# The last batch's rows leave in two pieces, and its gates are worked out ahead of other copies

## The chip, the cores and the metric

The kernel runs on one core of a Trainium2 chip. TensorE (PE) multiplies matrices into PSUM banks; VectorE (DVE) and ScalarE (ACT) read those banks and do the elementwise work; GpSimd (POOL) mostly issues DMAs here, among them all indirect ones; SyncE (SP) issues DMAs alone, and ACT can issue them too. Each engine works through its own instructions in the order in which they were written down. The metric is the device time of one execution in microseconds, the median of several.

## The reference

First chunked attention: 4 batches, 8 heads, 768 positions of 64 numbers, in chunks of 32 queries that see a window of 56 keys and 8 memory slots. Its result is laid out as 3,072 rows of 512. Then a mixture of 8 experts with two layers (512 to 1,024 to 512), in which each row goes to the two experts with the largest noisy logits:

```python
x = np.ascontiguousarray(attn_out.transpose(0, 2, 1, 3)).reshape(B * S, H * D)
logits = x @ w_gate
noisy_logits = logits + np.log1p(np.exp(x @ w_noise)) * noise
top2 = np.argpartition(-noisy_logits, 2, axis=1)[:, :2]
top2_w = np.exp(top2_l - top2_l.max(-1, keepdims=True))
top2_w /= top2_w.sum(-1, keepdims=True) + 1e-09
...
h = np.maximum(x[mask] @ w1[e], 0.0)
out[mask] += top2_w[mask, k, None] * (h @ w2[e])
```

## The kernel before

**Attention.** Sixteen pairs of heads (`NPAIR`, four to a batch) go through one software pipeline: transposes of q and k, scores, maximum, exponential, the product with v, and the division that writes the pair's columns into `xrow`, a tile of 128 partitions x 6 x 264 words per batch. A row of it has `XC` = 256 words for the 512 bf16 numbers and 8 words for the gates. `xT_pe` transposes a pair's columns on PE and copies them on ACT (tile `xt`); `logits_pe` multiplies `xt` with both gate matrices into `bankL`.

**Routing.** When a batch has its logits, `route(b)` gives a list of groups of steps. `s1` makes the noise scale (`ns`, two ACT instructions), `s1b` the noisy logits (`nl`), `s2` and `s2b` count for each expert how many beat it (`over`) and keep the two best (`two`, `mm_all`); `s3` ranks the rows by two-step prefix sums on PE; `s2c` and `s2d` make the exponentials (`gd` on DVE, `ge` on ACT); `s4` normalises them into the gates, stores them in the last 8 words of `xrow` and writes the batch's rows to `x_rows` in DRAM (L422); `s4b` and `s5` turn ranks into slots (`rk`, `r_all`, `past`, `tl`), `s5b` (`Rn`, DVE) and `s5c` (`col`, GpSimd) make the one-hot factors, `s6` multiplies them on PE, `s7` adds to the table `tab`. `decode` makes row numbers of the table: `idx_s` after batch 1, `idx_a` after batch 2, `idx_f` (with `idx_h`) after batch 3, the last.

**Experts.** The work is cut into ten sets: four tiles of 128 rows each for experts 0 and 1, filled from the first batches, then those experts' remaining three tiles, then seven tiles each for experts 2 to 7 (the seventh tile of an expert has 64 rows). For each set GpSimd gathers rows from `x_rows` by index (L604), `turn` transposes a tile on PE and copies it and its gate, `up` multiplies by w1 and `relu` evicts to `hts` or `htf`, `down` multiplies by w2, evicts with the gate as factor to `ys`, and GpSimd adds the rows to `out` by an indirect DMA (L676). The first scatter of a set waits until all of the set before has landed. `every()` is a generator over this; `units(k)` runs k of its yields (a yield is one block of 128 of the 1,024 hidden columns in `up`, or one tile in `down`), `until(mark)` runs it to a mark. `cnt["by"]` says which engine evicts: DVE, ACT, or both in turn.

**Order.** It is written out by hand: instructions stand on each engine as the program calls them. At the end of attention the last batch's routing is threaded through the first two sets, whose first halves were gathered by `idx_s` and whose second halves by `idx_a`. The groups of `route(B - 1)` run with (3, 4, 1, 4, 1) yields behind them, and three yields ahead. After the last group comes `decode` to `idx_f`, and then the gathers of all that is left. Tiles in DRAM carry dependencies: a batch's row write goes through a view of its own (`xd_part`), and gathers read through the whole of `x_rows`, so a gather waits for the row writes issued before it, and a row write for the gathers issued before it.

**Overflow.** Rows that find no slot are counted at the end; for them the gates are read back from `x_rows` (tile `gov`, L850, on SyncE), multiplied by what was missed and written back (L873), and a loop that normally does not run handles them.

Of the kernel before, what the change touches and what calls it, by code (L numbers as in the profile page):

```python
# [12 lines left out]
F32 = mybir.dt.float32  # L13
# [11 lines left out]
def kernel(  # L25
# [14 lines left out]
    nc = tc.nc  # L40
    B, H, S, D = q.shape
# [8 lines left out]
    NP = N // 128  # L50
# [9 lines left out]
    NT = 7  # L60
# [28 lines left out]
    def body():  # L89
# [231 lines left out]
        def mult_dve(n):  # L321
# [6 lines left out]
            nc.vector.reciprocal(rec.rearrange("p x u (h o) -> p x u h o", o=1), po[:, :, :, :, D:D + 1])  # L328
            nc.vector.tensor_tensor(out=xr, in0=po[:, :, :, :, :D], in1=rec.rearrange("p x u (h o) -> p x u h o", o=1).to_broadcast([128, 2, UB, 2, D]), op=Alu.mult)  # L329

        logits = {}

        def xT_pe(n):
            b, hp = divmod(n, HP)
            p_x = bf16v(tr(), BT, 128)
            for t in range(BT):
                nc.tensor.transpose(out=p_x[:, t, :], in_=xrows[b][:, t, hp * 64:(hp + 1) * 64].bitcast(BF16), identity=identb)
            xt = ap_.tile([128, BT, 128], BF16, name="xt")
            nc.scalar.copy(xt, p_x)
            st[n]["xt"] = xt  # L340

        def logits_pe(n):
            b, hp = divmod(n, HP)
            if hp == 0:
                logits[b] = f32v(bankL, BT, 2 * E)
            for t in range(BT):
                nc.tensor.matmul(out=logits[b][:, t, :], lhsT=st[n]["xt"][:, t, :], rhs=wgn[:, hp, :],
                                 start=(hp == 0 and t == 0), stop=(hp == KP - 1), skip_group_check=True)
# [5 lines left out]
        def route(b):  # L354
# [61 lines left out]
            def s4():  # L416
                ge, gs = R["ge"], T("gs", [128, BT])
                nc.vector.tensor_mul(ge, ge, R["two"])
                nc.vector.tensor_reduce(out=gs, in_=ge, axis=AX, op=Alu.add)
                nc.vector.reciprocal(gs, gs)  # L420
                nc.vector.tensor_tensor(out=xrows[b][:, :, XC:].bitcast(F32), in0=ge, in1=bc(gs, E), op=Alu.mult)
                (nc.sync if b < B - 1 else nc.scalar).dma_start(out=xd_part[b][b * S:(b + 1) * S].rearrange("(t p) r -> p t r", p=128), in_=xrows[b])  # L422

            def s4b():
                sh = [128, BT, 2, E]
# [62 lines left out]
                    nc.vector.tensor_add(seen[:, :EARLY], seen[:, :EARLY], gap)  # L488

            if b == B - 1:  # L490
                return (s1,), (s1b, s2), (s2b, s3, s2c, s4b, s5, s5c), (s2d,), (s4, s5b), (s6, s7)
            if b == B - 3:
                return (s1,), (s1b, s2), (s2b, s2c, s2d), (s3, s4, s4b, spare_a), (s5, s5c, spare_b), (s5b, spare_c), (s6, s7, s8, spare_d, begin_first)
            return (s1,), (s1b, s2), (s2b, s2c, s2d), (s3, s4, s4b), (s5, s5c), (s5b,), (s6, s7, s8)
# [239 lines left out]
        def units(k):  # L734
            for _ in range(k):
                next(moe, None)

        def until(*mark):
            for at in moe:
                if at == mark:  # L740
                    return
            assert False, mark
# [68 lines left out]
            zero_fill(8 * x, 8)  # L811
        load_w2(1)
        logits_pe(NPAIR - 2)
        xT_pe(NPAIR - 1)
        cnt["by"] = "dve"
        for j in range(FIRST):
# [1 line left out]
        logits_pe(NPAIR - 1)  # L818
        begin, *rest = route(B - 1)
        begin[0]()  # L820
        units(3)
        cnt["by"] = "act"
        for g, more in zip(rest, (3, 4, 1, 4, 1)):
            for fn in g:
                fn()
            units(more)
# [11 lines left out]
        actx.close()  # L838
        pools["full"] = ctx.enter_context(tc.tile_pool(name="full", bufs=1))
        lp = ctx.enter_context(tc.tile_pool(name="lp", bufs=1))  # L840
        until("down", NS - 4, NT - 1)


# [2 lines left out]
        sh = [128, NP, 2, E]  # L846
        miss = lp.tile(sh, F32, name="miss")
        nc.vector.tensor_tensor(out=miss, in0=mm_all, in1=o12.rearrange("p t (k o) -> p t k o", o=1).to_broadcast(sh), op=Alu.mult)
        gov = lp.tile([128, NP, E], F32, name="gov")
        nc.sync.dma_start(out=gov, in_=xd[:, XC:].rearrange("(t p) e -> p t e", p=128).bitcast(F32))  # L850
        nc.vector.tensor_add(miss[:, :, 0], miss[:, :, 0], miss[:, :, 1])
        nc.vector.tensor_mul(gov, gov, miss[:, :, 0])
        ov = lp.tile([128, NP], F16, name="ov")
# [108 lines left out]
```

## Time and profile before

| | |
|---|---|
| median of 3 runs | 346.19 us (344.0 to 346.33) |
| profiled execution: time, span | 343.07 us, 341.3 us |
| mean granted TensorE clock | 0.918 |
| PE busy | 274.3 us (80%) |
| GpSimd busy | 229.3 us (67%) |
| DVE busy, ACT busy | 161.2 us, 149.5 us |

In the profile's lines an instruction is given by its start (us from the start of the span), its length, engine, source line, operation and tiles, and in brackets the time for which its engine had stood idle, with what released it. A lower case q behind an engine (ACTq) marks the engine's queue as the issuer of a DMA. Attention fills the first 112 us; the last batch's routing lies between 113 and 134 us; experts alone run from there on.

### The profile page before, as it was taken

The numbers are of one execution on the slowest core, as the hardware profiler recorded it, in microseconds if no ns is written. First come the engines' busy times: TensorE is split into PE (matmuls) and PEld (weight loads), VectorE is DVE, ScalarE is ACT, GpSimd is POOL, SyncE is SP. The second block draws the span as 40 slices with busy tenths as digits, with TensorE's granted clock in tenths as the row PEclk, the third lists the DMA queues.
The fourth block names the chain that finished last, engine by engine and source line by source line (L and its number), as shares of the span: only waits on it lengthen the run. The fifth ranks groups of instructions, "written<-read, shape, count | busy, mean of one in ns | idle before, by whom it ended". The sixth has DMA issues, their size and how long they took to land. (4 is left out here: it accounts for less than half of the span.)

```text
span 341.3 us, 7625 instructions
## 1 busy us (share of the span) xinstructions
PE 274.3 (80%) x3071; PEld 174.2 (51%) x3085; DVE 161.2 (47%) x363; ACT 149.5 (44%) x295; POOL 229.3 (67%) x219
## 2 busy tenths in 40 slices
PE   0777677878548667799999999999999999999900
PEld 0656566666436555345565555555555555455400
DVE  7457659779876465222434333342332633134100
ACT  1688988878355544123343433423423333132200
POOL 8997767737443250687788887887888784848281
PEclk9969978969695999899999999999999999999965
DMA  9999999999979999469999999999999999959395
GB/s 108 161 154 187 167 161 166 212 133 194 196 143 309 398 286 203 79 103 185 247 152 198 172 240 197 239 195 194 206 160 205 216 148 157 147 74 130 40 131 70
DMA packets 99110, 60.30 MB, mean 177 GB/s; under 512 B 63488, under 2 KB 83968, under 8 KB 99072
## 3 DMA queue, kind: packets, MB, share of 16 engines
q0 software_dynamic: 82208, 49.84, 106.5%
q1 hardware_dynamic: 15792, 9.05, 9.2%
q10 hardware_dynamic: 1072, 0.88, 0.8%
q8 instruction: 26, 0.43, 0.5%
q14 instruction: 12, 0.10, 0.1%
HBM read 65.07 MB, written 23.27 MB: 259 GB/s over the span
## 5 line engine op out<-in xcount | busy, mean ns | idle before, releaser
L676 POOL DMA_INDIRECT out_dram<-ys,idx_f x40 | 62.8, 1570 | 26.6 <-issue 14.8
L648 PEld LDWEIGHTS <-w1t 128*128 128x128 bf16 x576 | 56.3, 99 | 40.4 <-issue 5.1
L604 POOL DMA_INDIRECT xl<-x_rows,idx_f x48 | 50.0, 1041 | 26.7 <-DVE hts L633 11.2
L664 PE MATMUL bankE<-w2t,htf 128*128 128x512 bf16 x278 | 65.7, 379 | 0.5
L675 DVE TENSOR_SCALAR ys<-bankE,gt 128x512 f32<-128x512 f32 (+1 forms) x32 | 21.9, 684 | 63.3 <-PE bankE L664 49.8
L648 PE MATMUL bankE<-xTf,w1t 128*128 128x416 bf16 x256 | 50.6, 339 | 0.0
L673 ACT ACTIVATE ys<-bankE,gt 128x512 f32<-128x512 f32 x24 | 16.5, 688 | 68.1 <-PE bankE L664 59.3
L134 POOL DMA_DIRECT2D vp<-in_v_dram x34 | 33.4, 989 | 15.5 <-PE bankO L317 4.3
L664 PEld LDWEIGHTS <-htf 128*128 128x128 bf16 x288 | 27.2, 98 | 28.8 <-issue 0.2
L633 DVE TENSOR_SCALAR htf<-bankE 128x416 bf16<-128x416 f32 x32 | 18.9, 591 | 26.7 <-PE bankE L648 26.7
L631 ACT ACTIVATE htf<-bankE 128x416 bf16<-128x416 f32 x32 | 16.5, 517 | 27.1 <-PE bankE L648 27.1
L264 ACT COPY kT<-bankT 64x768 bf16<-64x768 bf16 x32 | 25.3, 791 | 6.5 <-PE bankT L254 6.2
L648 PE MATMUL bankT<-xTf,w1t 128*128 128x416 bf16 x128 | 27.8, 339 | 0.2 <-DVE htf L633 0.2
L621 PE MATMUL bankT<-identb,xl 128*128 128x128 bf16 (+1 forms) x224 | 20.5, 220 | 5.7 <-DMA xl<-x_rows,idx_f 2.4
L621 PEld LDWEIGHTS <-xl 128*128 128x128 bf16 (+1 forms) x224 | 15.4, 100 | 16.2 <-issue 4.4
L664 PE MATMUL bankE<-w2t,hts 128*128 128x512 bf16 x92 | 22.7, 395 | 0.2
L288 DVE TENSOR_REDUCE mx<-bankS 128x12 f32<-128x768 f32 x16 | 15.2, 953 | 9.1 <-PE bankS L283 9.1
L314 PE MATMUL bankO<-memv,PT 128*128 128x132 bf16 x96 | 10.2, 256 | 9.5 <-ACT PT L307 9.3
L648 PE MATMUL bankE<-xTs,w1t 128*128 128x256 bf16 (+1 forms) x104 | 14.9, 283 | 2.6 <-DVE xTs L625 1.3
L456 POOL TENSOR_TENSOR col<-mm_all,tl 128x672 f16<-128x672 f16 x4 | 6.7, 1672 | 14.6 <-DVE tl L443 14.6
L329 DVE TENSOR_TENSOR xrow<-bankO,rec 128x768 bf16<-128x768 f32 x16 | 15.3, 958 | 1.9 <-DMA x_rows<-xrow 1.4
L290 DVE TENSOR_TENSOR sd<-bankS,mx 128x768 f32<-128x768 f32 x16 | 15.3, 958 | 1.8 <-DVE mx L288 0.5
(182 smaller groups left out, 453.6 us busy)
## 6 DMA issues: line engine op xcount, KB each, us to landing
w1t<-in_moe_w_dram POOLq DMA_DIRECT2D x8, 1024.0 KB, 11.3
w2t<-in_moe_w_dram POOLq DMA_DIRECT2D x8, 1024.0 KB, 10.7
out_dram<-zt SPq DMA_DIRECT2D x3, 2048.0 KB, 10.2
vp<-in_v_dram POOLq DMA_DIRECT2D x30, 168.0 KB, 8.6
qg<-in_q_dram POOLq DMA_DIRECT2D x16, 192.0 KB, 7.7
kg<-in_k_dram POOLq DMA_DIRECT2D x16, 192.0 KB, 8.2
x_rows<-xrow SPq DMA_DIRECT2D x3, 792.0 KB, 8.4
x_rows<-xrow ACTq DMA_DIRECT2D x1, 792.0 KB
```

The source lines that it names most:

```text
L134: nc.gpsimd.dma_start(out=vp[p0 + j:p0 + j + nj, c:c + m, hh, :], in_=bass.AP(v.tensor, v.offset + (hd * S + c * chunk + j - left_ctx) * D ...
L264: nc.scalar.copy(kbufs[n % 2][hs, hh].rearrange("d (p j) -> d p j", j=SJ), p_t[hs])
L290: nc.vector.tensor_tensor(out=sd, in0=st[n]["ps"], in1=mx.rearrange("p x (u o) -> p x u o", o=1).to_broadcast([128, 2, BT, CTX]), op=Alu.s ...
L604: nc.gpsimd.indirect_dma_start(out=xl, out_offset=None, in_=xd, in_offset=bass.IndirectOffsetOnAxis(ap=idx[:, c:c + 1], axis=0), bounds_ch ...
L621: nc.tensor.transpose(out=p_t[:, kp, :w], in_=xl[:w, kp * 64:(kp + 1) * 64].bitcast(BF16), identity=identb[:w, :w])
L631: nc.scalar.activation(out=dst, in_=src, func=Act.Relu)
L633: nc.vector.tensor_scalar(out=dst, in0=src, scalar1=0.0, scalar2=None, op0=Alu.max)
L648: nc.tensor.matmul(out=h[:, :hi - lo], lhsT=W1[e][:, kp, f * 128:(f + 1) * 128], rhs=xTs[s][:, kp, lo:hi], start=(kp == 0), stop=(kp == KP ...
L664: nc.tensor.matmul(out=y, lhsT=ht[:, f, o:o + w], rhs=W2[e][:, f, :], start=(f == 0), stop=(f == FB - 1))
L673: nc.scalar.activation(out=ys[:, :wide], in_=y[:, :wide], func=Act.Copy, scale=gate)
L675: nc.vector.tensor_scalar(out=ys[:, :wide], in0=y[:, :wide], scalar1=gate, scalar2=None, op0=Alu.mult)
L676: ins = nc.gpsimd.indirect_dma_start(out=rows, out_offset=bass.IndirectOffsetOnAxis(ap=idx, axis=0), in_=ys[:, :wide], in_offset=None, bou ...
```

## The change

- The last batch's rows leave in two pieces. The 512 numbers of a row (words 0 to `XC`) are written by ACT right behind the logits of pair 14, ahead of the copy of `xt` for pair 15; the 8 gate words are written by ACT where the whole row was written before.
- In the last batch's routing `s2d` (the exponential) stands in the group with the selection, and the yields between the groups become (2, 4, 0, 0) instead of (3, 4, 1, 4, 1), so that the table comes after 9 yields of the threaded work and not after 16. The three yields ahead of the groups are evicted by ACT, no longer by DVE.
- The read of the gates for the overflow part moves from SyncE's queue, on which little else stands, to ACT's, where it comes behind the evictions of the sixth set's down tiles; in the program it now stands one set earlier, with its tile.

```diff
+        def put_rows(eng, b, lo, hi):
+            eng.dma_start(out=xd_part[b][b * S:(b + 1) * S, lo:hi].rearrange("(t p) r -> p t r", p=128), in_=xrows[b][:, :, lo:hi])
...
-                (nc.sync if b < B - 1 else nc.scalar).dma_start(out=xd_part[b][b * S:(b + 1) * S].rearrange("(t p) r -> p t r", p=128), in_=xrows[b])
+                if b < B - 1:
+                    put_rows(nc.sync, b, 0, ROW)
+                else:
+                    put_rows(nc.scalar, b, XC, ROW)
...
-                return (s1,), (s1b, s2), (s2b, s3, s2c, s4b, s5, s5c), (s2d,), (s4, s5b), (s6, s7)
+                return (s1,), (s1b, s2), (s2b, s3, s2c, s2d, s4b, s5, s5c), (s4, s5b), (s6, s7)
...
         logits_pe(NPAIR - 2)
+        put_rows(nc.scalar, B - 1, 0, XC)
         xT_pe(NPAIR - 1)
         cnt["by"] = "dve"
         for j in range(FIRST):
...
         begin, *rest = route(B - 1)
         begin[0]()
+        cnt["by"] = "act"
         units(3)
-        cnt["by"] = "act"
-        for g, more in zip(rest, (3, 4, 1, 4, 1)):
+        for g, more in zip(rest, (2, 4, 0, 0)):
             for fn in g:
                 fn()
             units(more)
...
+        until("down", NS - 5, NT - 1)
+        gov = lp.tile([128, NP, E], F32, name="gov")
+        nc.scalar.dma_start(out=gov, in_=xd[:, XC:].rearrange("(t p) e -> p t e", p=128).bitcast(F32))
         until("down", NS - 4, NT - 1)
...
-        gov = lp.tile([128, NP, E], F32, name="gov")
-        nc.sync.dma_start(out=gov, in_=xd[:, XC:].rearrange("(t p) e -> p t e", p=128).bitcast(F32))
```

## The prediction

> **What bounds the kernel now.** I read the engine shares first, then the windows, then GpSimd's timeline, and last the ends of the result tiles. From 140 us on the work is experts only, and two engines look full:
>
> ```profile
> 200.00:240.00 40.00, 39.79 (x261) 21.73 (x262) 13.69 (x25) 13.26 (x36) 32.94 (x27) 1.00 1.10 208
> ```
>
> The columns are the stretch, the busy time of PE, weight loads, DVE, ACT and GpSimd (POOL), the granted clock, the DMA share and GB/s. PE has 0.2 us free in 40. GpSimd shows 32.9, but its timeline says what the remaining 7 are:
>
> ```profile
> 138.35 1.13 POOL L604 DMA_INDIRECT xl<-x_rows,idx_f  x1 [11.25 <-DVE hts L633]
> ...
> 146.37 1.63 POOL L676 DMA_INDIRECT out_dram<-ys,idx_a  x1 [0.30 <-issue]
> ...
> 152.96 1.57 POOL L676 DMA_INDIRECT out_dram<-ys,idx_a  x1 [0.31 <-issue]
> ...
> 166.40 1.63 POOL L676 DMA_INDIRECT out_dram<-ys,idx_a  x1 [0.30 <-issue]
> ```
> ```profile
> 321.92 1.55 POOL L676 DMA_INDIRECT out_dram<-ys,idx_f  x1 [6.54 <-issue]
> ...
> 333.07 1.55 POOL L676 DMA_INDIRECT out_dram<-ys,idx_h  x1 [0.30 <-issue]
> ```
>
> Between its instructions stands 0.30 us of issue, so GpSimd's queue is full from 138.35 to 334.6, but for a few waits for transfers to land (the 6.54 is the first scatter of the last set, which must wait until the set before has landed). Which of the two full engines sets the end is told by when the tiles to scatter are ready:
>
> ```profile
> 139.88 0.75 DVE L675 TENSOR_SCALAR ys<-bankE,gt 128x512 f32<-128x512 f32 x1 [1.30 <-PE bankE L664]
> ```
> ```profile
> 150.43 0.69 ACT L673 ACTIVATE ys<-bankE,gt 128x512 f32<-128x512 f32 x1 [1.01 <-remote]
> ```
> ```profile
> 152.48 0.75 DVE L675 TENSOR_SCALAR ys<-bankE,gt 128x512 f32<-128x512 f32 x1 [1.54 <-PE bankE L664]
> ```
> ```profile
> 324.15 0.48 DVE L675 TENSOR_SCALAR ys<-bankE,gt 128x256 f32<-128x256 f32 x1 [2.03 <-PEq L885]
> ```
>
> The last tile is ready at 324.6 and scattered at 333.07, 8.4 us late; the first tile of the second set is ready at 153.2 and scattered at 166.40. So the scatters trail the tiles: the end hangs on GpSimd's queue, and what moves its start at 138.35 moves the end as much. The one place where PE comes close is the first set of four: its first tile is ready at 140.6 for a scatter at 146.37 (5.7 us), its fourth at 151.1 for 152.96, so it has 1.5 us beyond the 0.3 of issue.
>
> What holds 138.35? The gathers need the index tile and the last batch's rows in x_rows:
>
> ```profile
> 133.58 0.22 DVE L547 TENSOR_TENSOR idx_f<-row,emp 128x56 int32<-128x56 f32 x1
> ```
> ```profile
> 129.65 0.41 ACTq L422 DMA_DIRECT2D x_rows<-xrow  x1
> ```
> ```profile
> 137.76 0.37 SPq L850 DMA_DIRECT2D gov<-x_rows  x1
> ```
>
> The index is there at 133.8; the row write starts at 129.65, and SyncE's read of the same rows, which waits for it, goes at 137.76. The write took 8.1 us, GpSimd starts 0.6 later, and the profile's "DVE hts" at 138.35 is only the last thing that ended. PE also feels it: it runs out of work after its first down tile.
>
> ```profile
> 137.95 1.89 PE L664 MATMUL bankE<-w2t,hts 128*128 128x512 bf16 x7
> 141.78 0.40 PE L621 MATMUL bankT<-identb,xl 128*128 128x128 bf16 x4 [1.94 <-DMA xl<-x_rows,idx_f]
> ...
> 143.07 3.09 PE L664 MATMUL bankE<-w2t,hts 128*128 128x512 bf16 x8
> ```
> ```profile
> 142.00:144.00 2.00, 1.51 (x11) 0.79 (x8) 0.42 (x1) 0.63 (x2) 1.39 (x3) 0.52 0.30 85
> ```
>
> From the end of the first down tile (139.84) to the end of the second (146.16) it takes 6.3 us, part of it at a granted clock of 0.52. That is what the change can save.
>
> **The early piece.** The write of 1,024 of each row's 1,056 bytes now stands on ACT's queue ahead of the copy of xt for the last pair. It must not overtake earlier readers of x_rows: the program makes it wait for the gathers by idx_s and all four by idx_a, which read through the whole of x_rows. Before, the same waits stood at 129.65, when they were long over. The last of the four:
>
> ```profile
> L604 POOL DMA_INDIRECT xl<-x_rows,idx_a x2: 1011/1013/1015, 119.6 to 120.9; - x2
> ...
> DMA to landing us min/median/max: 6.3/6.3/6.3
> ```
> ```profile
> 126.02 0.40 PE L621 MATMUL bankT<-identb,xl 128*128 128x128 bf16 x4 [1.07 <-DMA xl<-x_rows,idx_a]
> ```
>
> 120.9 + 6.3 = 127.2; PE's own wait for the second of the four until 126.02 agrees. Nothing that the change does comes before these gathers, so they land where they did. ACT, however, wants to issue this write at about 117.3:
>
> ```profile
> 117.37 0.80 ACT L339 COPY xt<-bankT 128x768 bf16<-128x768 bf16 x1 [0.16 <-PE bankT L337]
> 118.77 0.21 ACT L362 ACTIVATE ns<-bankL 128x48 f32<-128x48 f32 x1 [0.61 <-PE bankL L347]
> 119.01 0.24 ACT L363 ACTIVATE ns<-ns 128x48 f32<-128x48 f32 x1
> ```
>
> That a write waits on ACT and holds what is behind it, the old kernel shows: the issue at 129.65 waits there for the gates, and until the eviction behind it had run PE had no bank:
>
> ```profile
> 130.54 0.60 PE L648 MATMUL bankE<-xTs,w1t 128*128 128x256 bf16 x4 [0.68 <-ACT hts L631]
> ```
>
> The Trainium skill, "DMA: Bandwidth & Descriptors", section "Anatomy of one DMA", states the same: a DMA's semaphore wait is served by the issuing sequencer, not by the DMA engines; the row above agrees, and a sum by this rule is the one that follows.
>
> So ACT stands from 117.3 to 127.2, then issues for 0.41 (row of 129.65), and xt starts at 127.7 instead of 117.37: 10.3 us late. Queued behind it on ACT are xt, both ns and all evictions; PE stands before the last logits, which need xt, and its up-pieces and rank matmuls wait behind those.
>
> **What is won back.** ns comes 1.4 after xt: 129.1, and 0.3 more for a slow PE: 129.4. Then DVE:
>
> ```profile
> 121.03 0.20 DVE L369 TENSOR_TENSOR nl<-ns,nz_all 128x48 f32<-128x48 f32 x1
> ...
> 123.27 0.19 DVE L387 TENSOR_SCALAR two<-over 128x48 f16<-128x48 f32 x1
> ...
> 125.37 0.25 DVE L443 TENSOR_TENSOR tl<-tl,tokv 128x84 f16<-128x84 f16 x1
> 128.71 0.21 DVE L418 TENSOR_TENSOR ge<-ge,two 128x48 f32<-128x48 f32 x1 [3.09 <-ACT ge L402]
> ```
>
> nl stood until 121.03 behind three evictions that are now ACT's, so it starts 0.5 after ns, at 129.9 (8.9 late); `two` is ready 2.4 later, 132.3. The rank matmul on PE needs it, and has five up-pieces ahead (three and two), which start 2 after xt, at 129.7. A piece takes 0.44 at full clock and 0.89 at half:
>
> ```profile
> 119.18 0.60 PE L648 MATMUL bankT<-xTs,w1t 128*128 128x256 bf16 x4 [0.45 <-DVE gt L626]
> 119.62 1.04 PE L648 MATMUL bankE<-xTs,w1t 128*128 128x256 bf16 x8
> ...
> 123.51 0.18 PE L407 MATMUL bankT<-two,upper 128*128 128x48 f16 x1 [1.55 <-DVE two L387]
> ```
> ```profile
> 106.91 3.57 PE L648 MATMUL bankT<-xTs,w1t 128*128 128x256 bf16 x16 [1.10 <-ACT xTs L623]
> ```
>
> PE fell to half clock here after 1.9 us of idleness, so after 10 it is at half. All five fast end at 131.9 (then `two` decides), all five slow at 134.2; I take 133.3, between them. By the Trainium skill, "TensorE: Matmul & The Clock Gate", section "What's actually happening", about 3.4 us of sustained work release the clock; by that rule nearly four pieces are slow and they end at 133.6, 0.3 more than I take. The slow tile of 143.07 took 1.2 more than the 1.89 of the one before it, so there the half clock ended within some 2.5 to 3 us.
>
> Rank matmul at 133.3 instead of 123.51; tl ends 2.1 after it (123.51 to 125.62): 135.4. The gates' first step, which had waited 3.09 us for ge behind evictions, follows at once: 135.4 instead of 128.71, 6.7 late. The same steps follow as before, so idx_f is there at 133.8 + 6.7 = 140.5.
>
> The gates' write, 24 KB in 768 pieces of 32 bytes, stands on ACT behind three pieces, two gathered tiles and one piece more: 133.3 + 0.3 for the rank matmuls + 1.3 + 2.0 (two transposes and copies, 132.43 to 134.44 below) + 0.4 + 0.4 for its eviction = 137.7. Its price has no row; from both sides:
>
> ```profile
> x_rows<-gov SPq DMA_DIRECT2D x1, 96.0 KB, 6.7
> ...
> wgn_f<-in_moe_w_gate_dram SPq DMA_DIRECT2D x1, 16.0 KB, 2.0
> wgn_f<-in_moe_w_noise_dram SPq DMA_DIRECT2D x1, 16.0 KB, 3.1
> ```
>
> 512 such pieces took 2.0 and 3.1, 3,072 took 6.7, the whole rows 8.1. I take 3.1, nearest in size: landed 140.8. The big piece (8.1 from 127.3) is in by 135.4. With the 0.6 of GpSimd the gathers start at 141.4 instead of 138.35: **3.0 us late**.
>
> PE has fewer pieces ahead of the index now and 15 behind it: seven, two transposes with their copies, eight:
>
> ```profile
> 132.34 0.16 PE L831 MATMUL bankT<-half,fold 64*128 64x8 f16 x1
> 132.43 0.72 PE L621 MATMUL bankT<-identb,xl 128*128 128x128 bf16 x8
> 134.44 1.05 PE L648 MATMUL bankE<-xTs,w1t 128*128 128x256 bf16 x8 [1.29 <-DVE xTs L625]
> ```
>
> Fold at 132.34 + 6.7 = 139.0; 7 x 0.44 = 3.1, transposes 2.0 (132.43 to 134.44), eight pieces 3.5 (134.44 to 137.95): first down tile at 147.7 instead of 137.95. Now the gathers are ahead of it, so its stall goes: two transposes (0.6) and 1.9 per tile end the second at 152.1 instead of 146.16, **5.9 late**. The fourth tile is then ready at 151.1 + 5.9 = 157.0 and scattered at 157.3 instead of 152.96: **4.3 late**, more than the gathers' 3.0, and by the 1.5 of slack above less than PE's 5.9. Every later scatter has 8 us and more, so 4.3 reaches the end.
>
> **The rest.** The gates' read for the overflow part leaves SyncE at 137.76, where it lay beside the first gathers (GpSimd issues those at a fixed pace, so nothing is won), and goes to ACT a whole expert ahead of the one use of its data. It costs ACT 0.4 us of issue where ACT is busy 13 us of 40 (the first row above). Bounds: 0, and 1 us if its 3,072 small pieces, 6.7 us in the table, hold back a landing that GpSimd waits for. I take 0.
>
> Sum against the profiled run: 343.07 (span 341.3) + 4.3 = 347.4. That run is 3.1 below the median; on the median: 346.19 + 4.3 = **350.5 us**.
>
> **Rivals.**
> 1. ACT isn't held: the waits of the early write are over when it is reached, or ACT goes past it. Then nl starts at 119.3; the rank work is bounded by the second idx_a tile in PE's queue at 126.02; one copy and one piece later the table is made, idx_f at 130, gates landed by 130.7, gathers at 131.3, 7 early. PE's first tile, 0.8 early and without its 3.8 us of stall, lets the first scatter go at 140.1, 6.3 early: 339.9, faster. For it: the stall at 141.78 is real. Against it: the landing at 127.2 and the row at 130.54. It decides if the gathers land by 117. The Trainium skill, "DMA: Bandwidth & Descriptors", section "Rules for kernel authors", says to issue a DMA early and wait for it late; by that rule this rival would be the case, and no row here bears it out for a write that has readers before it. Chance 0.09.
> 2. ACT is held, but PE makes up more (full clock, fewer gaps), so that only the gathers' delay is left: 2 to 3.4 us, 348.2 to 349.6. Against it: 5.9 would have to fall to 4.9. Chance 0.18.
> 3. ACT is held, and the gates' write takes what whole rows take, 8.1: gathers at 146.4, 8.0 late, 354.2; or half clock lasts on through the pieces behind the index (7 x 0.45 more), 353.6. For it: every write here ends with a landing in DRAM, and 6.7 is in the table for a small one. Chance 0.15.
> 4. My forecast, 348.5 to 352.5: 0.58.
>
> **How the numbers follow.** Within 1% is what this kernel's runs can't tell apart: up to 349.6. A fifth of the forecast's own chance and all of rival 2 lie there: 0.11 + 0.18 = 0.29. Slower takes the rest of the forecast and rival 3: 0.47 + 0.15 = 0.62. Faster is rival 1: 0.09. The range reaches over rival 2 and rival 3's price, 347 to 355, and leaves out rival 1 and the ends of the others.
>
> **What would show it.** ACT idle some 10 us ahead of the xt copy, released by the early write's issue near 127.2, and PE idle as long; no wait of 3 us at the first use of ge; the first gather near 141; PE without the gap after its first down tile; the first set's scatters waiting for ys. Wrong: xt at 117 as before, or a first gather before 138.

## The result, and the profile after

| | before | after |
|---|---|---|
| median | 346.08 us (344.0 to 346.33) | 356.32 us (355.55 to 357.43) |
| ratio, 95% interval | | 1.0315 [1.0281, 1.0348] |
| profiled execution: time, span | 343.07, 341.3 us | 357.43, 355.5 us |

Slower by 10.2 us; the forecast was 4.3 slower, and its range ended at 355. The direction came as forecast, and so did the hold of ACT; the size is more than twice the forecast's.

First, two traces have to be set on one another. The first gather by `idx_a` stands ahead of everything that the change touches. Before, then after, GpSimd's timeline:

```profile
116.82 1.12 POOL L604 DMA_INDIRECT xl<-x_rows,idx_a  x1 [7.23 <-DVE idx_a L547]
```
```profile
119.90 1.12 POOL L610 DMA_INDIRECT xl<-x_rows,idx_a  x1 [7.11 <-DVE idx_a L553]
```

This execution was 3.1 us late before the change could act; over all profiled runs below, this gather starts between 113.65 and 120.28. So all instants below are counted from this gather, and called "+11.2" and so on. After it, ACT's timeline and PE's (start, length, engine, line, operation, and in brackets the idle time with its releaser):

```profile
130.62 0.41 ACTq L332 DMA_DIRECT2D x_rows<-xrow  x1
131.13 0.80 ACT L342 COPY xt<-bankT 128x768 bf16<-128x768 bf16 x1 [10.85 <-DMA xl<-x_rows,idx_a]
```
```profile
131.98 0.58 PE L627 MATMUL bankT<-identb,xl 128*128 128x128 bf16 x4 [11.26 <-ACT xt L342]
```

That is the forecast's picture: the early write issues at +10.7, ACT has stood 10.85 us, released by a gather by `idx_a`, `xt` starts at +11.2 (before +0.55), and PE has stood 11.26 us for it. At the other end, GpSimd's timeline again:

```profile
145.70 1.13 POOL L610 DMA_INDIRECT xl<-x_rows,idx_f  x1 [4.65 <-DVE idx_h L555]
...
158.79 1.63 POOL L682 DMA_INDIRECT out_dram<-ys,idx_a  x1 [5.37 <-ACT gt L632]
...
165.38 1.57 POOL L682 DMA_INDIRECT out_dram<-ys,idx_a  x1 [0.30 <-issue]
```

The first gather by `idx_f` waits for the index now, not for rows. Behind six gathers GpSimd stands 5.37 us ahead of the first scatter, because no `ys` is ready; before it stood only the 0.30 of issue there. The fourth scatter starts at +45.5, before at +36.1: 9.3 late. Later sets do not win this back: the last scatter of all is 11.4 late.

The change was run three times with a profile (once here, twice beside experiments below), which shows what in the sum is steady:

| instant, us behind the first gather by `idx_a` | before | forecast | after | again (e14) | again (e16) |
|---|---|---|---|---|---|
| `xt` of the last pair | 0.55 | 10.9 | 11.2 | 12.7 | 12.8 |
| rank matmul | 6.7 | 16.5 | 17.5 | 18.6 | 18.6 |
| fold (table done on PE) | 15.5 | 22.2 | 24.0 | 25.0 | 25.0 |
| first gather by `idx_f` | 21.5 | 24.6 | 25.8 | 26.8 | 26.8 |
| first down tile | 21.1 | 30.9 | 35.4 | 34.6 | 34.5 |
| fourth scatter | 36.1 | 40.5 | 45.5 | 44.7 | 44.6 |

(The forecast's column is its clock time less 116.82.) No one step failed by 5 us. On the way to the fourth scatter each step was short, in the first execution by 0.3 to 2.7 us, and all on the same side. The two repeats lost 2.5% (2.8 to 3.5 was expected of e14), the first comparison 3.15%.

### The profile page after: what moved, and what is told of

Its sections match the earlier page's. It is cut to its first block, busy times and chain, and to the rows that moved or that the text cites. A ratio compares the mean times of both kernels' runs of the same rounds, so it can differ in the third digit from the quotient of the medians.

```text
span 355.5 us, 7627 instructions
## 1 busy us (share of the span) xinstructions
PE 279.8 (79%) x3071; PEld 177.7 (50%) x3085; DVE 163.1 (46%) x364; ACT 149.0 (42%) x294; POOL 229.2 (64%) x219
## 5 line engine op out<-in xcount | busy, mean ns | idle before, releaser
L654 PEld LDWEIGHTS <-w1t 128*128 128x128 bf16 x576 | 57.9, 102 | 48.5 <-issue 8.2
L679 ACT ACTIVATE ys<-bankE,gt 128x512 f32<-128x512 f32 x24 | 16.5, 688 | 66.9 <-PE bankE L670 48.5
L639 DVE TENSOR_SCALAR htf<-bankE 128x416 bf16<-128x416 f32 x32 | 18.9, 592 | 26.8 <-PE bankE L654 23.1
L627 PE MATMUL bankT<-identb,xl 128*128 128x128 bf16 (+1 forms) x224 | 20.0, 220 | 12.9 <-ACT xt L342 11.3
L637 ACT ACTIVATE htf<-bankE 128x416 bf16<-128x416 f32 x32 | 16.5, 517 | 29.9 <-PE bankE L654 25.5
L627 PEld LDWEIGHTS <-xl 128*128 128x128 bf16 (+1 forms) x224 | 15.5, 100 | 22.6 <-issue 15.1
L670 PE MATMUL bankE<-w2t,hts 128*128 128x512 bf16 x92 | 21.5, 379 | 0.2
L288 DVE TENSOR_REDUCE mx<-bankS 128x12 f32<-128x768 f32 x16 | 15.2, 952 | 12.7 <-PE bankS L283 7.7
L654 PE MATMUL bankE<-xTs,w1t 128*128 128x256 bf16 (+1 forms) x104 | 17.7, 317 | 3.1 <-ACT xTs L629 2.3
L314 PE MATMUL bankO<-memv,PT 128*128 128x132 bf16 x96 | 10.2, 257 | 12.4 <-ACT PT L307 11.2
L342 ACT COPY xt<-bankT 128x768 bf16<-128x768 bf16 x16 | 12.8, 799 | 13.8 <-DMA xl<-x_rows,idx_a 10.8
L682 POOL DMA_INDIRECT out_dram<-ys,idx_a x8 | 12.7, 1589 | 7.5 <-ACT gt L632 5.4
```

The source lines that it names most:

```text
L288: nc.vector.tensor_reduce(out=mx, in_=st[n]["ps"], axis=AX, op=Alu.max)
L627: nc.tensor.transpose(out=p_t[:, kp, :w], in_=xl[:w, kp * 64:(kp + 1) * 64].bitcast(BF16), identity=identb[:w, :w])
L637: nc.scalar.activation(out=dst, in_=src, func=Act.Relu)
L639: nc.vector.tensor_scalar(out=dst, in0=src, scalar1=0.0, scalar2=None, op0=Alu.max)
L654: nc.tensor.matmul(out=h[:, :hi - lo], lhsT=W1[e][:, kp, f * 128:(f + 1) * 128], rhs=xTs[s][:, kp, lo:hi], start=(kp == 0), stop=(kp == KP ...
L670: nc.tensor.matmul(out=y, lhsT=ht[:, f, o:o + w], rhs=W2[e][:, f, :], start=(f == 0), stop=(f == FB - 1))
```

## The experiments

Ratios are to the kernel before on the same chip in the same comparison; the last three columns are instants of the profiled execution, counted as above.

| run | ratio, 95% interval | first gather by `idx_f` | first down tile | fourth scatter |
|---|---|---|---|---|
| before | 1 | 21.5 | 21.1 | 36.1 |
| e1_sync | 1.0019 [0.9984, 1.0054] | 21.3 | 22.8 | 35.9 |
| e2_yields_only | 1.0025 [0.9984, 1.0066] | 21.7 | 21.3 | 36.4 |
| e3_split_only | 1.0272 [1.0190, 1.0355] | 28.6 | 32.5 | 44.0 |
| e4_gov_only | 0.9981 [0.9934, 1.0028] | 21.2 | 20.8 | 35.9 |
| e5_free | 0.9971 [0.9938, 1.0003] | 20.9 | 21.1 | 35.5 |
| e9_free_old_yields | 0.9988 [0.9959, 1.0017] | 19.5 | 22.5 | 34.1 |
| e18_act_late | 1.0009 [0.9980, 1.0038] | 22.0 | 20.9 | 36.6 |
| e10_w2_later | none (one execution) | 16.6 | 21.0 | 38.4 |
| e11_free_w2 | 0.9915 [0.9876, 0.9953] | 14.9 | 20.8 | 30.9 |
| e12_before_w2 | 0.9992 [0.9961, 1.0023] | 17.1 | 20.8 | 32.6 |
| e13_sync_w2 | 0.9957 [0.9925, 0.9990] | 16.4 | 21.1 | 31.9 |
| e8_act_evicts | 1.0254 [1.0198, 1.0311] | 25.9 | 32.1 | 42.2 |
| e14_after_again | 1.0252 [1.0185, 1.0318] | 26.8 | 34.6 | 44.7 |
| e16_after_5 | 1.0251 [1.0210, 1.0291] | 26.8 | 34.5 | 44.6 |
| e17_act_evicts_5 | 1.0229 [1.0192, 1.0266] | 26.9 | 34.5 | 44.6 |
| e15_warm | 1.0143 [1.0094, 1.0192] | 26.7 | 33.6 | 43.7 |

### Which part of the change costs

The expectations name theories by letters: A is the hold of ACT, D that the landing of the rows' and gates' writes is held by other transfers on the DMA engines, F that DVE's evictions stand behind the table's decode. The parts one by one: e1_sync is the whole change with the early piece on SyncE, on which nothing else waits:

```diff
         logits_pe(NPAIR - 2)
-        put_rows(nc.scalar, B - 1, 0, XC)
+        put_rows(nc.sync, B - 1, 0, XC)
         xT_pe(NPAIR - 1)
```

> The changed kernel, with the early piece of the last batch's rows issued by SyncE and no longer by ACT. The same semaphores are waited for, but on a queue with nothing behind it. Theory A (the write's wait for the idx_a gathers holds ACT and with it PE) expects: no stall of 10 us ahead of the last xt copy, first idx_f gather 10 to 12 us earlier than in the changed kernel measured from that copy, and about 338 to 343 us, faster than before. Theory B (9 threaded yields in place of 16 leave PE short ahead of the table and pile pieces up behind it) expects 349 to 353 us, since the yields are as changed. Theory C (the gates' read for the overflow part disturbs the experts at its new place) expects 350 us or more.

e2_yields_only is the kernel before with the new groups, yields and evictions, and the rows in one piece:

```diff
-                return (s1,), (s1b, s2), (s2b, s3, s2c, s4b, s5, s5c), (s2d,), (s4, s5b), (s6, s7)
+                return (s1,), (s1b, s2), (s2b, s3, s2c, s2d, s4b, s5, s5c), (s4, s5b), (s6, s7)
...
+        cnt["by"] = "act"
         units(3)
-        cnt["by"] = "act"
-        for g, more in zip(rest, (3, 4, 1, 4, 1)):
+        for g, more in zip(rest, (2, 4, 0, 0)):
```

> The kernel before with only the moved exponential and the new yields (2, 4, 0, 0), with ACT as evictor of the first three; whole rows are written at the old place, and the overflow read is as before. Theory A expects no stall, the row write some 3 us earlier than before (the wait for ge goes), and 342 to 346 us. Theory B expects 349 us or more. Theory C expects 346 us.

e3_split_only is the kernel before with the rows in two pieces, both on ACT, and the old groups and yields:

```diff
-                (nc.sync if b < B - 1 else nc.scalar).dma_start(out=xd_part[b][b * S:(b + 1) * S].rearrange("(t p) r -> p t r", p=128), in_=xrows[b])
+                if b < B - 1:
+                    put_rows(nc.sync, b, 0, ROW)
+                else:
+                    put_rows(nc.scalar, b, XC, ROW)
...
         logits_pe(NPAIR - 2)
+        put_rows(nc.scalar, B - 1, 0, XC)
         xT_pe(NPAIR - 1)
```

> The kernel before with only the split write (early piece on ACT, gates later), old yields, old place of the exponential, old overflow read. Theory A expects the whole stall: xt of the last pair some 10 us late behind the early piece, PE idle as long, and 350 to 356 us. Theory B expects 346 us or a little less, theory C 346 us.

e4_gov_only is the kernel before with the read for the overflow part moved as in the change:

```diff
+        until("down", NS - 5, NT - 1)
+        gov = lp.tile([128, NP, E], F32, name="gov")
+        nc.scalar.dma_start(out=gov, in_=xd[:, XC:].rearrange("(t p) e -> p t e", p=128).bitcast(F32))
         until("down", NS - 4, NT - 1)
...
-        gov = lp.tile([128, NP, E], F32, name="gov")
-        nc.sync.dma_start(out=gov, in_=xd[:, XC:].rearrange("(t p) e -> p t e", p=128).bitcast(F32))
```

> The kernel before with only the overflow part's gates read moved to ACT and one set earlier. Theories A and B expect 345 to 347 us, no change. Theory C expects 349 us or more.

The split alone loses what the whole change loses; order and read lose nothing that can be measured. ACT's timeline of e3_split_only:

```profile
131.05 0.41 ACTq L332 DMA_DIRECT2D x_rows<-xrow  x1
131.56 0.80 ACT L342 COPY xt<-bankT 128x768 bf16<-128x768 bf16 x1 [10.90 <-DMA xl<-x_rows,idx_a]
```

And e1_sync, ACT's line and SyncE's:

```profile
119.68 0.80 ACT L342 COPY xt<-bankT 128x768 bf16<-128x768 bf16 x1 [0.16 <-PE bankT L340]
```
```profile
130.07 0.37 SPq L332 DMA_DIRECT2D x_rows<-xrow  x1
```

Here the first gather by `idx_a` stands at 119.13, so the same write waits on SyncE until +10.9, as long as on ACT, and `xt` is on time. The wait did not go away; it holds nobody now. The gain that theory A expected (338 to 343 us) is missing: the run's median is 347.94 us beside 346.97 of the kernel before.

### No wait at all

e5_free leaves the early write on ACT where the change puts it, and takes its reason to wait: the gathers by `idx_s` and `idx_a`, which never name a row of the last batch, read under a name of their own and wait for the row writes of the batches before. e9_free_old_yields is the same with the old groups, yields and read.

```diff
-                    out=xl, out_offset=None, in_=xd, in_offset=bass.IndirectOffsetOnAxis(ap=idx[:, c:c + 1], axis=0),
+                    out=xl, out_offset=None, in_=xd_part[B] if early else xd, in_offset=bass.IndirectOffsetOnAxis(ap=idx[:, c:c + 1], axis=0),
...
+                if early:
+                    for b in range(B - 2 if idx is idx_s else B - 1):
+                        tc.add_manual_dep(g.ins, wrote[b].ins.name, mybir.DependencyInfo(mybir.DependencyClass.Sync, mybir.DependencyReason.DATA), reason="rows of the first batches")
```

> The changed kernel, with the gathers by idx_s and idx_a reading x_rows through a view that is declared apart from the last batch's rows (those gathers hold only rows of the first three batches), and ordered by hand behind those batches' writes. So the early piece, still on ACT, waits for no reader. Theory A (only the wait held things up) expects: no stall of ACT; the early piece issued at the place where it stands and landed before the index is ready; the first idx_f gather some 14 to 16 us behind the first idx_a gather, where e1_sync had 21.3 and the kernel before 21.5; 340 to 344 us. Theory D (the landing of the rows is set by the DMA engines, which are full with the zero fill and a weight load until then, so issuing it early moves little) expects the first idx_f gather at 19 us or later and 345 to 348 us.

> The kernel before with the split write and the early gathers' view of e5_free, and the old yields, exponential and overflow read. Theory A expects the index to be last (17 us behind the first idx_a gather), the first idx_f gather at 17 to 18.5 and 343 to 345.5 us, some 2 us slower than e5_free. Theory D expects 20 us or later and 346 to 348 us.

ACT's timeline of e5_free (first gather by `idx_a` at 114.97), and GpSimd's:

```profile
114.99 0.41 ACTq L334 DMA_DIRECT2D x_rows<-xrow  x1
115.53 0.80 ACT L344 COPY xt<-bankT 128x768 bf16<-128x768 bf16 x1 [0.16 <-PE bankT L342]
...
125.78 0.39 ACTq L334 DMA_DIRECT2D x_rows<-xrow  x1
```
```profile
135.86 1.13 POOL L613 DMA_INDIRECT xl<-x_rows,idx_f  x1 [12.20 <-DVE hts L645]
```

The loss is gone, so the hold is its cause. But the gain is missing too. The rows left at +0.0, the 24 KB of gates at +10.8, the index was there at +13.1, and still the gathers started at +20.9. (In e9_free_old_yields the index came at +18.3 and the gathers at +19.5, between what the two theories expected.) What differs from the changed kernel, which issued the gates at 141.41 and had them landed by 145.70, is the company. Windows of e5_free (the last two columns are the DMA share, 1.00 being 16 busy engines, and GB/s):

```profile
126.00:128.00 2.00, 1.43 (x8) 0.98 (x9) 1.41 (x8) 0.10 (x1) 0.00 (x0) 0.63 1.12 299
128.00:130.00 2.00, 2.00 (x11) 1.43 (x10) 1.07 (x4) 0.38 (x1) 0.00 (x0) 0.51 1.13 267
...
132.00:134.00 2.00, 1.40 (x13) 1.36 (x14) 0.60 (x2) 1.02 (x3) 0.00 (x0) 1.00 1.17 162
134.00:136.00 2.00, 2.00 (x21) 1.78 (x20) 0.94 (x3) 0.92 (x3) 0.14 (x1) 1.00 0.03 3
```

The DMA engines are full until about 134 and the gathers start as they empty. The profile counts packets by queue. The gates' write is 784 packets on ACT's queue (q10); the weight load is on GpSimd's (q0). Here is the changed kernel from 142 to 143, then e5_free from 131 to 133 (packets, MB, share of the 16 engines):

```profile
q10 hardware_dynamic: 784, 0.02, 37.2%
```
```profile
q0 software_dynamic: 357, 0.37, 113.0%
q10 hardware_dynamic: 356, 0.01, 24.2%
```

Alone, all 784 packets went within that 1 us, 1.6 us behind the issue at most. In e5_free they went between 130 and 135, behind the rows of the same queue (until about 129) and then packet for packet with the load: 356 small ones beside 357 of 1 KB. So the write took some 9 us from its issue at 125.78.

### One queue, another place

e18_act_late keeps the early write on ACT, with its wait, behind the last pair's routing steps:

```diff
-        put_rows(nc.scalar, B - 1, 0, XC)
...
             units(more)
+            if more == 4:
+                put_rows(nc.scalar, B - 1, 0, XC)
```

> The early write on ACT, later in its queue: behind xt, ns, the exponential and six evictions, ahead of the gates' write. It still may not start before the last gather by idx_a has landed, 10.9 us behind the first. If only what stands behind it on ACT matters, ACT reaches it at about 9 to 10 and is held for 2 us at most: xt at 0.55, first gather by idx_f at 20.5 to 22 as before, ratio 0.997 to 1.006. If a write that waits on ACT costs by itself, whatever stands behind it, the ratio stays above 1.01.

ACT's timeline (first gather by `idx_a` at 114.83):

```profile
115.37 0.80 ACT L342 COPY xt<-bankT 128x768 bf16<-128x768 bf16 x1 [0.16 <-PE bankT L340]
...
125.49 0.38 ACT L637 ACTIVATE hts<-bankE 128x256 bf16<-128x256 f32 x1 [0.59 <-PE bankE L654]
127.22 1.03 ACTq L332 DMA_DIRECT2D x_rows<-xrow  x2
```

The write issues at +12.4, as late as the held one (+10.7, and +12.2 and +12.3 in the repeats), on the same engine, and costs nothing (1.0009): ACT comes to it at 125.9, when little is left to wait for. What counts is the place in the queue.

### Who holds the landing

The load of expert 1's second weights, 1 MB, is issued by GpSimd just behind the gathers by `idx_a`. Four runs put it behind gathers by `idx_f` (e10_w2_later, with e1_sync: behind the first three; the others: behind all six, on e5_free, on the kernel before, and on e1_sync):

```diff
-        load_w2(1)
         logits_pe(NPAIR - 2)
...
             todo.extend((s, j) for j in sets[s][1])
+        load_w2(1)
```

> e1_sync with the load of w2 for expert 1 moved on GpSimd from behind the idx_a gathers to behind the first three idx_f gathers, so that it does not run beside the row write; PE will wait for it later. Theory D expects the row write, issued 10.9 us behind the first idx_a gather, to land in some 4 us in place of 9, and the first idx_f gather at 15 to 17 us in place of 21.3. If the write's own landing takes that long without company, the gather stays at 20 to 21. The total tells nothing here.

> The new order with the rows' early piece on ACT not held (the gathers by idx_s and idx_a read through a name of their own and wait for the rows' writes alone, as in the run before), and the load of expert 1's second weights moved behind the six gathers by idx_f. The same result is computed. If the landing of the gates' write was held by the 1-MB weight load that shares the DMA engines (theory D), the gates' write issued about 10.8 us behind the first gather by idx_a lands within 4 to 5 us, and the first gather by idx_f starts 14.5 to 16.5 us behind that gather instead of 20.9 in the run with the load in its place; the first scatter starts near 25 to 26 instead of 29, and the time falls by 3 to 5 us, ratio to before about 0.985 to 0.995. If the landing was held by something else (the zero fill, the many 32-byte pieces themselves), the gather stays at 19 or later and the ratio within 0.5% of 1. Rival on the other side: the weight load now lands beside the gathers and expert 1's first down tile waits for it, so the scatters of the second set start late; then the ratio is 1.00 or above though the first gather is early.

> The kernel before with that load moved alone. Theory D: the whole rows, issued 12.8 us behind the first gather by idx_a as before, land in about 4 us instead of 8.1; the first gather by idx_f starts at 17 to 18.5 instead of 21.5 and the time falls by up to 3 us (ratio 0.990 to 1.000). If the load isn't what holds the rows' write, the gather stays at 21 and the ratio at 1.000 within 0.4%.

> The new order with the rows' early piece on SyncE's queue, and the load moved. The early piece waits for the gathers by idx_a until about 11 us behind the first of them, on a queue that holds no compute. Theory D: it and the gates' write, issued at the same time, land together within 4 to 6 us, the first gather by idx_f starts at 15.5 to 17 instead of 21.3, and the time falls by 2 to 4 us (ratio 0.987 to 0.997). Otherwise the gather stays at 20 or later and the ratio at 1.00.

ACT's and GpSimd's timelines of e11_free_w2 (first gather by `idx_a` at 116.93), and its windows:

```profile
116.94 0.41 ACTq L334 DMA_DIRECT2D x_rows<-xrow  x1
...
127.75 0.39 ACTq L334 DMA_DIRECT2D x_rows<-xrow  x1
```
```profile
131.82 1.05 POOL L613 DMA_INDIRECT xl<-x_rows,idx_f  x1 [6.21 <-DVE hts L645]
```
```profile
128.00:130.00 2.00, 1.43 (x12) 0.98 (x9) 1.25 (x7) 0.07 (x1) 0.00 (x0) 0.50 0.59 158
130.00:132.00 2.00, 2.00 (x16) 1.59 (x15) 1.24 (x5) 0.56 (x2) 0.18 (x1) 0.76 0.01 1
```

The gates' write, issued at +10.8 as in e5_free, has landed by +14.9 and no longer by +20.9: 6 us from the place of one load. In all four runs the gathers come 4 to 6 us earlier than without the move. e11_free_w2 is faster than the kernel before by 0.85% (338.72 against 341.38 us), the best of the study. The bill comes at expert 1's first down tile, which needs those weights. PE's timelines of e11_free_w2 and e12_before_w2:

```profile
150.03 6.22 PE L676 MATMUL bankE<-w2t,hts 128*128 128x512 bf16 x28 [3.82 <-DMA w2t<-in_moe_w_dram]
```
```profile
149.53 6.74 PE L664 MATMUL bankE<-w2t,hts 128*128 128x512 bf16 x23 [6.03 <-DMA w2t<-in_moe_w_dram]
```

So the lead shrinks: e11's fourth scatter is 5.3 us early and its second set 4.2 (+45.3 against +49.6), e12's 3.6 and 2.0. The times show less still: 2.7 us by medians, where 3 to 5 was expected, and 0.2 for e12, where up to 3 was. Single profiled executions can't say where the remaining 1 to 2 us went; e11's, at 341.70 us, lay 3.0 above its run's median. In e10_w2_later PE waited 6.07 us for rows of the gathers behind the load, and its one time, 342.58 us, lies on the kernel before.

### The size of the loss

What stood behind the table was the forecast's largest miss in the first profiled execution. PE's timeline after:

```profile
143.90 0.16 PE L838 MATMUL bankT<-half,fold 64*128 64x8 f16 x1 [0.57 <-DVE half L836]
143.99 0.61 PE L654 MATMUL bankT<-xTs,w1t 128*128 128x256 bf16 x4
144.44 1.70 PE L654 MATMUL bankE<-xTs,w1t 128*128 128x256 bf16 x8
146.07 1.01 PE L654 MATMUL bankT<-xTs,w1t 128*128 128x256 bf16 x4
146.87 1.62 PE L654 MATMUL bankE<-xTs,w1t 128*128 128x256 bf16 x8
148.34 0.60 PE L654 MATMUL bankT<-xTs,w1t 128*128 128x256 bf16 x4
...
150.57 1.03 PE L654 MATMUL bankE<-xTs,w1t 128*128 128x256 bf16 x8 [1.19 <-ACT xTs L629]
...
154.82 0.60 PE L654 MATMUL bankE<-xTs,w1t 128*128 128x256 bf16 x4 [0.80 <-ACT hts L637]
155.26 1.89 PE L670 MATMUL bankE<-w2t,hts 128*128 128x512 bf16 x7
```
```profile
140.00:142.00 2.00, 0.60 (x4) 0.29 (x3) 1.97 (x3) 1.14 (x5) 1.04 (x1) 1.00 0.00 0
...
146.00:148.00 2.00, 2.00 (x11) 1.38 (x10) 0.47 (x3) 0.38 (x1) 1.70 (x2) 0.50 0.22 53
```

The seven pieces take 4.8 us (143.99 to 148.77, where the transposes begin), not 3.1: a granted clock of 0.50 (the third number from the end of a window), a second time. PE had been warm again (1.00 at 140 to 142), but the new order gives it no yields beside `Rn` and the table, and it idles there, 0.60 us busy in those 2. The eight pieces behind the transposes took 4.7 us (150.57 to 155.26), not 3.5, at full clock and with 0.80 us of waiting for an eviction; in the repeats they took 3.5, and what made them long here is open.

Two suspects for the seven pieces, half clock and DVE's evictions queued behind the table's decode, were first moved together without intent by e8_act_evicts, which leaves the evictions of those seven pieces to ACT:

```diff
             todo.extend((s, j) for j in sets[s][1])
+        units(7)
         cnt["by"] = "both"
```

> The changed kernel, with the seven up-pieces behind the table evicted by ACT alone, so that none of their evictions stands on DVE behind the nine steps that decode the table. Theory F (those evictions behind the decoding are what made the pieces take 4.8 us where 3.1 were forecast) expects the first down tile 1.0 to 1.7 us earlier measured from the first idx_a gather (35.4 in the changed kernel) and 354.5 to 355.5 us. Theory G (PE's half clock made them slow) expects less than 0.5 us and 356 to 357 us.

Its first down tile came at +32.1, but its granted clock was 1.00 throughout that stretch:

```profile
140.00:142.00 2.00, 2.00 (x20) 1.79 (x19) 1.15 (x6) 1.55 (x5) 0.71 (x1) 1.00 0.00 0
```

So the engine and the clock were not told apart. Two controls and a kernel that keeps PE busy followed; e14_after_again and e16_after_5 are the changed kernel, e17_act_evicts_5 is e8_act_evicts. e15_warm adds matmuls that nobody reads:

```diff
         xT_pe(NPAIR - 1)
...
+        spin(44)
...
         for g, more in zip(rest, (2, 4, 0, 0)):
+            if g is rest[3]:
+                spin(6)
...
             units(more)
+        spin(2)
```

> The changed kernel once more, unchanged, so that the run with ACT's evictions (ratio 1.0254) stands beside two ratios of the changed kernel. Expected: ratio 1.028 to 1.035 again, the first down tile of the first set about 35 us behind the first gather by idx_a, PE at half clock in the stretch behind the index table. If the half clock there is an accident of one execution, it is missing here and the first down tile is at 33 or earlier.

> The changed kernel with extra matmuls on PE whose results nobody reads: 44 of 128x512 (0.24 us each at full clock, 10.4 us) while PE waits for the late xt, six ahead of the table's matmuls and two ahead of its fold, where PE waits for DVE. Evictions stay where they are. If half clock is what the forecast missed: granted clock 1.00 behind the hold and behind the table, the five pieces end before `two` is ready, so the rank matmul comes 16.1 us behind the first gather by idx_a instead of 17.5, the seven pieces behind the table take 3.1 instead of 4.8, the first down tile starts at 31.5 to 32.5 instead of 34.6 to 35.4 and the time is 2 to 3 us under the changed kernel's. If DVE's evictions are what sets the pace there, clock is 1.00 and the first down tile still stands at 33.5 or later.

> The changed kernel on the chip of this comparison: ratio 1.022 to 1.035, first down tile at 34.5 to 35.5 behind the first gather by idx_a.

> The changed kernel with ACT evicting the seven pieces behind the table, as in the run before, in more rounds. If DVE's evictions are a term of their own, 1 to 3 us under the changed kernel of the same call (ratio to before lower by 0.003 to 0.009) and the first down tile at 32 to 33 again; if the run before was quick by its clock alone, and half clock returns here, its first down tile is at 34 or later and its ratio is the changed kernel's.

Windows behind the table, of e16_after_5 and then of e15_warm:

```profile
138.00:140.00 2.00, 1.15 (x16) 0.89 (x17) 0.96 (x5) 0.00 (x0) 0.00 (x0) 0.80 0.07 4
140.00:142.00 2.00, 2.00 (x12) 1.35 (x10) 1.32 (x7) 0.38 (x1) 0.86 (x1) 0.50 0.00 0
142.00:144.00 2.00, 2.00 (x17) 1.67 (x16) 0.85 (x2) 0.58 (x2) 1.39 (x3) 0.85 0.25 68
```
```profile
130.00:132.00 2.00, 1.55 (x11) 1.04 (x8) 1.68 (x6) 0.84 (x3) 0.00 (x0) 0.59 1.03 126
...
140.00:142.00 2.00, 1.86 (x20) 1.25 (x16) 1.28 (x7) 0.11 (x1) 0.00 (x0) 1.00 0.04 8
142.00:144.00 2.00, 1.41 (x14) 1.11 (x13) 1.16 (x5) 0.66 (x2) 1.19 (x2) 1.00 0.00 0
```

The spin worked behind the table and not ahead of it: the 44 took 9.7 us, PE stood 3.6 us behind them until `xt` came, and the clock fell all the same (0.59), so nothing is learnt of the first half-clock stretch, and the rank matmul came at +18.5 instead of the 16.1 expected. From the fold to the first down tile, the three executions of the changed kernel take 11.4, 9.6 and 9.5 us, e17 9.4 with half clock back, e15 8.7, and e8, with full clock and ACT's evictions, 7.9. So it is the clock first; once it is full, DVE's evictions are next, as e15's PE shows:

```profile
142.88 0.60 PE L654 MATMUL bankT<-xTs,w1t 128*128 128x256 bf16 x4 [0.59 <-DVE hts L639]
```

The evictions alone are worth nothing that can be measured (1.0229 against 1.0251), and e8's lead over e17, the same kernel, goes with its clock. Idleness is what lets the clock fall, as e15 shows, but not in every execution: e8 stood idle beside the table nearly as long (gaps of 1.08, 1.20 and 0.58 us, in e16_after_5 1.08, 1.61 and 0.57) and kept it, and why is open. e3_split_only, held as long but with the old yields, kept 1.00 from 140 to 150. e15_warm's time is 3.7 us under the changed kernel's (0.0108 of 341.81; combining the two intervals, 1.5 to 5.9). Its trace explains 0.9 of this at the fourth scatter, and its second set starts where the changed kernel's does (+57.0, +56.9). Where the rest comes from is open.

## Why the prediction was wrong in size

The step that failed is the price of what follows the hold. From the fold to the first down tile the forecast took 8.7 us at full clock; it took 11.4 in the execution of the result, the largest miss there, because the clock fell a second time (1.7 us) and the eight last pieces took 1.2 us more. In the two repeats this step took 9.6 and 9.5, and the largest miss was the landing of the last gather by `idx_a`: 8.1 and 8.2 us, not 6.3.

**Right: the hold.** Who waits, for what, what is queued behind it and that PE stands with it came as written, and e3_split_only, e1_sync, e5_free and e18_act_late show it to be the cause, not only a companion. Rival 1's point of decision, that the gathers' landing must come before ACT gets there, was the right question.

**"120.9 + 6.3 = 127.2".** The landing of the last gather was taken from one row of one execution. Counted in the same way, from the start of that gather to the issue of the write, it took 6.7 us in the first execution (123.96 to 130.62) and 8.1 and 8.2 in the repeats, so `xt` came 0.3, 1.8 and 1.9 later than forecast. The price of a hold is a DMA's landing on full engines (DMA share 1.03 from 126 to 130 here), and one row doesn't give its spread.

**Five pieces to the rank matmul, 5.6 behind `xt`.** Measured 6.2, 5.9 and 5.8. In the first execution all five were slow, the forecast's outer bound. The Trainium skill's rule of about 3.4 us of work before the clock is released ("TensorE: Matmul & The Clock Gate", "What's actually happening") would, by the forecast's estimate, have added 0.3 to the value taken, 5.9 in all. The two repeats agree with that; the first execution, with half clock in all five pieces, took longer.

**"The same steps follow as before".** They followed, but not at the same length. GpSimd's timeline after, then DVE's, and the same step before:

```profile
139.74 1.30 POOL L462 TENSOR_TENSOR col<-mm_all,tl 128x672 f16<-128x672 f16 x1 [13.81 <-DVE ge L421]
```
```profile
140.18 0.94 DVE L424 TENSOR_TENSOR xrow<-ge,gs 128x48 f32<-128x48 f32 x1
141.03 1.75 DVE L456 TENSOR_TENSOR Rn<-rampm,slot 128x1536 f16<-128x1536 f16 x1
```
```profile
129.41 0.21 DVE L421 TENSOR_TENSOR xrow<-ge,gs 128x48 f32<-128x48 f32 x1
```

The gates' last step takes 0.94 us and ends as `col` ends on GpSimd (139.74 + 1.30 = 141.04); before, 2.3 us behind the end of `col`, it took 0.21. `Rn`, the table and the index come behind it, 0.7 late, in each execution in which the two overlap (e1_sync's row reads 0.94 too). The wait of 3.09 us for `ge`, which the forecast rightly let go, had kept these two apart. The Trainium skill, "SBUF — State Buffer", "Who interferes with whom", states that a DVE instruction with two SBUF inputs contends with a GpSimd instruction that reads SBUF, and that the lock is exclusive; these rows agree.

**"7 x 0.44 = 3.1" behind the table.** 4.8 in the first execution, 4.7 and 4.6 in the repeats. The forecast asked once whether PE is cold, behind the hold, and named "half clock lasts on" only in rival 3. It didn't last on: it came a second time, behind the idleness that the two zeros among the yields leave beside the table. Rival 3 had 3.1 more at this place by another cause; 1.7, 1.6 and 1.5 more were paid. In the repeats 0.7 of it came back in shorter transposes (1.3, not 2.0). In the first execution the eight pieces cost 1.2 more as well.

**The gates' write, 3.1 us.** It was through by 143.0, 1.6 us behind its issue (the 784 packets above), ahead of the need; rival 3's 8.1 fell. It was no bound there: by then the weight load was in, and the DMA share was 0.00 (the window of 140 to 142 above).

**First down tile to fourth scatter, 9.6 us.** Measured 10.1 in all three, on another path than the forecast's. It took the fourth tile as the bound, but that tile was ready at 164.3 for a scatter at 165.38. The first scatter came 3.5 us behind the first down tile, and from there to the fourth it took 6.6, as before (146.37 to 152.96).

Summed for the first execution: `xt` 0.3, up to the rank matmul 0.6, from there to the fold 0.8, to the first down tile 2.7, to the fourth scatter 0.5: with rounding 5.0 over the forecast's 4.3, 9.3 in all. For the second repeat: 1.9, 0.1, 0.8, 0.8 and 0.5: 4.1 over the forecast, 8.4 in all. The times were 10.2 and 8.6 us over the kernel before.

**"So 4.3 reaches the end."** That the fourth scatter's delay reaches the end as it is isn't shown. In the three executions it was 9.3, 8.5 and 8.4; at the first scatter of the second set 9.1, 7.4 and 7.3; at the last scatter of all 11.4, 11.3 and 9.4. e4_gov_only, whose time is that of the kernel before, was 0.3 early at the fourth scatter and 3.7 late at the last. So single executions differ in the later sets by as much as this, and the profiled execution of the kernel before lay 3.1 us under its median.

**"That is what the change can save".** It was wrong. Without the hold nothing is saved (e5_free, 0.9971): the gathers, and with them the stall of PE on the first set's second tile, are held by the landing of writes beside the 1-MB load. Rival 1's 6 us did not come from this change even without the hold; they came in part when the load went (first gather 6.6 us, fourth scatter 5.3 us early, time 2.7).

**The moved read, 0.** Right: 0.9981 with 1 in its interval.

## What to carry to other kernels

Before a DMA write is issued earlier, list what has read its destination before and still has to land, then ask what compute stands behind the write on the issuing queue: the wait is the same everywhere, but only a queue without urgent work behind it takes it for nothing. Before a write's landing is counted as moved, look at what else fills the DMA engines between its issue and its use; here a weight load that PE first used 12 us behind the gathers (150.54 against 138.35 in the kernel before) held them longer than the order of the writes did. When a pipeline is emptied once, price the clock and the idle gaps for every stretch that follows, not just for the first.

## What was not expected of the hardware

- A 24-KB write in 32-byte pieces was through 1.6 us behind its issue on idle DMA engines and after some 9 us beside a 1-MB load (e5_free), where the two queues moved 356 and 357 packets in the same 2 us. The Trainium skill, "DMA: Bandwidth & Descriptors", "Issuing engines are not separate DMA queues", states that transfers of all issuers interleave on the same 16 engines; these packet counts agree.
- One DVE instruction on 128x48 numbers took 0.94 us beside GpSimd's `col` and 0.21 without it.
- The granted clock fell twice within 25 us, and in e15_warm it fell behind 9.7 us of added matmuls and 3.6 us of idleness.
